# RWKV attention and a channel mixer in one kernel: three kinds of early VectorE work on GpSimd and ScalarE, and a weight request behind two products

## The chip, the cores and the metric

The kernel runs on one core of a Trainium2 chip. The metric is the device time of one execution in microseconds, lower is better. The engines are TensorE (PE; its weight loads are PEld), VectorE (DVE), ScalarE (ACT), GpSimd (POOL) and SyncE (SP), each with its own queue of instructions that it works through in order; they wait for each other by semaphores. Transfers are asked for by SyncE and GpSimd and run on 16 DMA engines.

## What is computed

A linear attention with a decaying state, and then an MLP mixer on its output, for 4 batches, 8 heads, 768 tokens and 48 elements per head (384 per token):

```python
for t in range(S):                                    # S = 768
    kt, vt, rt = (k[:, :, t], v[:, :, t], r[:, :, t])
    cur = np.einsum('bhd,bhe->bhde', u[None] * kt, vt)
    y[:, :, t] = np.einsum('bhd,bhde->bhe', rt, state + cur)
    state = w[None, :, :, None] * state + np.einsum('bhd,bhe->bhde', kt, vt)
...
xt = x.transpose(0, 2, 1)                             # x: y as (4, 768, 384)
h = np.maximum(xt @ w_tok1, 0.0) @ w_tok2             # 768 -> 256 -> 768 over the tokens
u = x + h.transpose(0, 2, 1)
h2 = np.maximum(u @ w_ch1, 0.0) @ w_ch2               # 384 -> 1536 -> 384 over the channels
return u + h2
```

## The kernel before

The tokens of each batch are cut into 6 units of 128, so there are 24 units; units 0 to 5 are the first batch. Attention within a unit is a product of scaled k and scaled r (the decay w is put into both by tables of its powers), masked to earlier tokens, times v; what came before the unit enters through a state matrix.

One unit u goes through these steps, each a short function that issues one or a few instructions:

- `kp`, `rp`: k and r, as loaded (`ld_k`, `ld_r`, f32 in SBUF), times their tables `wn` and `wp`, into the bf16 tile `kpr` (on GpSimd or VectorE). There are five such tiles, used in turn. `vb`: v as bf16 (ScalarE).
- `trk`, `trr`: four transposes each of the k half and the r half of `kpr`, into one PSUM tile `tr_ps` (TensorE).
- `rk`: `tr_ps` copied to SBUF (ScalarE). For units 0 to 4 and 6 it is two steps, `rkk` (k half, after `trk`) and `rkr` (r half, after `trr`); for others one step that issues both copies after `trr`.
- `at`: eight score matmuls into two PSUM tiles of four heads, `at_ps` 0 and 1 (TensorE). `AT0`, `AT1`: each of the two times the f32 mask, as bf16 into SBUF (VectorE). For units 0, 1, 5, 8 and 11 the second half goes another way: `raw` copies it from PSUM to bf16 (ScalarE), and `ATr` multiplies that by a bf16 mask (VectorE, both operands in SBUF).
- `pr`, `pg`, `yd`: the diagonal term (VectorE, four tiny matmuls into `g_ps`, VectorE or GpSimd). `pr` reads both halves of `rk`.
- `yS`, `y`: the state's part and the part within the unit, into `y_ps` (TensorE). `kv`, `S`: the state's update; in the third unit of a batch (unit 2 in the first) `S` uses the table `wGm`, which is built once from the constants `bm` and `wG`.
- `x`: `y_ps` plus `yd` into `x_b` (VectorE), the mixer's input.

When all six units of a batch are there, the mixer follows: `hid` and `hr` (token product and ReLU, `h_ps`, `h1r`), `ux`/`ub` or `bk`/`us` (second token product, added to x), then two halves of twelve `z` products with ReLU copies `zr` on ScalarE, and `h` products with `wch2`, `os` and the store. The `z` and `h` products of earlier batches are what TensorE does most of the time.

The order on each engine is not written by hand. `graph` makes all steps with their dependencies, ranks and estimated durations; `Plan.run` plays them through, gives each step an engine and a start, and sorts them; the kernel then issues them in that order. Two things are set behind it. `Plan.fill` puts idle matmuls (`fill_ps`) into TensorE's planned gaps. `products_in_turn` looks at the products of SBUF operands on VectorE and GpSimd, and where a GpSimd product stands at most 2.0 us behind one of VectorE's, it adds a wait of GpSimd's for VectorE. Every instruction passes through one helper, so the profile's line is the same for all, L515, and the tiles tell them apart; units are told by order.

The five weights come by seven GpSimd requests, which also turn f32 to bf16: `w0` and `w1` (the two token weights, tiles `wtok`), `w2`, `w6`, `w4` (first quarter, second quarter and second half of the columns of the first channel weight, `wch`), `w3` and `w5` (the second channel weight by halves of its rows). Their place on GpSimd is set by `wafter`. The loads of k, r and v stand on SyncE's queue; the first six units' are issued ahead of all else, and unit 6's k load waits for unit 5's y matmuls (`hold`).

Of the kernel before, what the change touches and what calls it, by code (L numbers as in the profile page):

```python
# [45 lines left out]
class Plan:  # L46
# [83 lines left out]
    def fill(self, since, until, least, margin, each, emit):  # L130

        mine = sorted((s for s in self.steps if s.engine == "PE"), key=lambda s: s.start)
        for a, b in zip(mine, mine[1:]):
            if b.start > until:
                break
            if a.end < since:
                continue
            taken = sum(1 for x in self.used if x[0] < b.start and x[1] > a.end)
            n = int((b.start - a.end - margin) / each)
            if b.start - a.end >= least and taken < self.banks and n > 0:  # L140
                s = self.add(f"fill{a.name}", [("PE", n * each, n * each)], emit=emit(n))
                s.engine, s.start, s.end, s.seen = "PE", a.end, a.end + n * each, a.end + n * each
        return sorted(self.steps, key=lambda s: s.start)


def products_in_turn(steps, apart):


    both = [s for s in steps if s.engine in ("DVE", "POOL") and s.name.rstrip("0123456789") in ("kp", "rp", "ku", "rku", "yd", "wGm")]
    dve = [s for s in steps if s.engine == "DVE"]  # L150
    behind, d = {}, None
    for s in both:
        if s.engine == "DVE":
            d = s if len(s.after) and s.name[:2] != "yd" or s.ways[0][0] == "POOL" else d
        elif d is not None and s.start - d.end < apart:
            n = dve.index(d)
            behind[s] = dve[n - 1] if n and d.start - dve[n - 1].end < 0.05 else d
            d = None
    return behind
# [9 lines left out]
def graph(do, cfg):  # L169
# [246 lines left out]
CFG = dict(apart=2.0,   # L416
    transfers=[("u", u) for u in range(0, 6)]
    + [('k', 6)]
    + [('r', 6)]
    + [('k', 7)]  # L420
    + [('r', 7)]
    + [('v', 6)]
    + [('v', 7)]
    + [('u', 8)]
# [20 lines left out]
    xload={6: 0.33},  # L445
    wtime=(3.0, 2.6, 1.55, 5.2, 3.1, 3.9, 1.55),
    raw=(0, 1, 5, 8, 11),
    rk_two=(0, 1, 2, 3, 4, 6),
    mix=(0.0, 0.0, -1.0, -2.6),
    off3=[{}, {}, {'AT0': -0.12, 'rp': 0.83, 'rku': 1.35}],  # L450
# [17 lines left out]
def kernel(  # L468
# [121 lines left out]
    for i in range(NB):  # L590
        t = const.tile([128, 2, H, P], bf16, name=f"kpr{i}")
# [24 lines left out]
    wGm = const.tile([128, HP, 2, D], f32, name="wGm")  # L616
# [387 lines left out]
    def do(kind, *args):  # L1004
        return lambda eng: STEPS[kind](eng, *args)

    def fill(eng, n):
        t = psM.tile([128, 512], f32, name="fill_ps", tag="m")
        for lo in range(0, n, 2):
            cols = slice(0, 256 * min(2, n - lo))  # L1010
            pe.matmul(t[:, cols], idle[:, 0:128], idle[:, cols], start=True, stop=True)

    plan = graph(do, CFG)
    steps = plan.run()
    if CFG.get("fill"):
        first = next(s for s in steps if s.name == "z0_0_0").start
        steps = plan.fill(CFG.get("fill_from", 0.0), first, *CFG["fill"], lambda n: lambda eng: fill(eng, n))
    behind = products_in_turn(steps, CFG["apart"])
    last = {}
    for s in steps:  # L1020
# [38 lines left out]
```

## Time and profile before

| | |
|---|---|
| Median of 3 runs | 165.36 us (164.93 to 165.66) |
| Profiled execution | 165.7 us, its span 164.0 us |
| Mean granted TensorE clock | 1.000 |
| Busy: TensorE / VectorE / ScalarE / GpSimd | 156.6 / 109.2 / 88.5 / 67.1 us |
| Moved by DMA | 26.26 MB, mean 160 GB/s |
| DMA packets under 512 B | 76665 of 87307 |

A row of the timeline reads: start and duration in us from the span's start, engine, line, operation, output<-inputs, shapes, how many in a row, and in brackets the idle time of the engine ahead of it and what ended it. The chain of waits has start, duration and what was waited for or done. In the page's slices one digit is a fortieth of the span, 4.1 us, and tells the busy tenths. A row of transfers tells the size of one and the time from its issue to its landing. A row of the windows tells the stretch, its length, the busy time of TensorE, its weight loads, VectorE, ScalarE and GpSimd (with the number of instructions), the granted clock, the DMA engines' busy share and GB/s.

### The profile page before, as it was taken

The numbers are of one execution on the slowest core, as the hardware profiler recorded it, in microseconds if no ns is written. First come the engines' busy times: TensorE is split into PE (matmuls) and PEld (weight loads), VectorE is DVE, ScalarE is ACT, GpSimd is POOL, SyncE is SP. The second block draws the span as 40 slices with busy tenths as digits, with TensorE's granted clock in tenths as the row PEclk, the third lists the DMA queues.
The fourth block names the chain that finished last, engine by engine and source line by source line (L and its number), as shares of the span: only waits on it lengthen the run. The fifth ranks groups of instructions, "written<-read, shape, count | busy, mean of one in ns | idle before, by whom it ended". The sixth has DMA issues, their size and how long they took to land.

```text
span 164.0 us, 3852 instructions
## 1 busy us (share of the span) xinstructions
PE 156.6 (95%) x1466; PEld 100.9 (62%) x1466; DVE 109.2 (67%) x225; ACT 88.5 (54%) x194; POOL 67.1 (41%) x83
## 2 busy tenths in 40 slices
PE   6798999999999999899999999999999999999992
PEld 3277865566677666566566565666656655666562
DVE  6679897602289889899899899977876582012021
ACT  3898662595488466789706450077253502914900
POOL 8748893000037848566875856204750000000000
DMA  4999999999798997999999972999990028012012
GB/s 92 221 223 207 173 154 173 192 194 232 153 231 233 190 213 220 196 238 180 217 231 133 263 135 67 203 231 194 194 240 4 0 53 216 19 52 96 0 48 96
DMA packets 87307, 26.26 MB, mean 160 GB/s; under 512 B 76665, under 2 KB 87290, under 8 KB 87290
## 3 DMA queue, kind: packets, MB, share of 16 engines
q1 hardware_dynamic: 83392, 22.88, 65.1%
q0 software_dynamic: 3888, 3.15, 13.1%
q8 instruction: 11, 0.18, 0.4%
q14 instruction: 6, 0.05, 0.2%
q10 hardware_dynamic: 10, 0.00, 0.0%
HBM read 20.65 MB, written 4.72 MB: 155 GB/s over the span
## 4 chain that ended last, share of the span: by engine, by line
PE 85%; DVE 5%; ACT 5%; issue 2%; POOL 1%; DVEq 0%; ACTq 0%
PE h_ps L515 33%; PE z_ps L515 29%; PE y_ps L515 5%; PE at_ps L515 5%; PE tr_ps L515 4%; PE hT_ps L515 3%; PE kv_ps L515 3%; ACT rk L515 2%; DVE AT L515 2%; DVE x_b L515 1%; PE w_ps L515 1%; DVE yd L515 1%; POOL kpr L515 1%; ACT wp L515 1%; ACT raw L515 1%
## 5 line engine op out<-in xcount | busy, mean ns | idle before, releaser
L515 ACT ACTIVATE zr<-z_ps 128x384 bf16<-128x384 f32 x94 | 45.4, 492 | 44.2 <-PE z_ps L515 44.1
L515 PE MATMUL z_ps<-uT,wch 128*128 128x384 bf16 x288 | 52.5, 326 | 0.2
L515 PE MATMUL h_ps<-wch,zr 128*128 128x384 bf16 (+1 forms) x300 | 52.5, 320 | 0.0
L515 PEld LDWEIGHTS <-zr 128*128 128x128 bf16 x300 | 27.9, 98 | 15.5 <-issue 0.2
L515 PEld LDWEIGHTS <-wch 128*128 128x128 bf16 x288 | 26.7, 98 | 16.1 <-issue 0.4
L515 POOL TENSOR_TENSOR yd<-vb,adg 128x384 f32<-128x384 bf16 x18 | 15.5, 859 | 42.2 <-ACT adg L515 25.1
L515 DVE TENSOR_TENSOR AT<-at_ps,mask 128x512 bf16<-128x512 f32 x43 | 27.9, 683 | 0.6 <-PE at_ps L515 0.5
L515 DVE TENSOR_TENSOR osb<-u_sb,h_ps 128x384 f32<-128x384 bf16 (+1 forms) x22 | 11.7, 532 | 23.5 <-PE h_ps L515 23.4
L515 POOL TENSOR_TENSOR kpr<-ld_r,wp 128x384 bf16<-128x384 f32 x16 | 17.0, 1064 | 5.3 <-DVE yd L515 2.2
L515 ACT COPY rk<-tr_ps 128x512 bf16<-128x512 bf16 x28 | 15.5, 589 | 5.5 <-PE tr_ps L515 5.1
L515 PEld LDWEIGHTS <-kpr 128*128 128x128 bf16 x192 | 13.6, 108 | 6.1 <-POOL kpr L515 2.6
L515 DVE TENSOR_TENSOR x_b<-y_ps,yd 128x384 bf16<-128x384 f32 x24 | 13.3, 552 | 5.8 <-PE y_ps L515 5.5
L515 POOL TENSOR_TENSOR kpr<-ld_k,wn 128x384 bf16<-128x384 f32 x15 | 15.5, 1031 | 2.1 <-PE z_ps L515 1.1
L515 PEld LDWEIGHTS <-rk 48*128 48x128 bf16 (+1 forms) x272 | 11.1, 100 | 6.4 <-issue 2.8
L515 PE MATMUL tr_ps<-ident,kpr 128*128 128x128 bf16 x112 | 12.3, 247 | 2.0 <-ACT rk L515 1.0
L515 ACT CAST vb<-ld_v 128x384 bf16<-128x384 f32 x24 | 12.3, 511 | 3.5 <-DMA ld_v<-in_v_dram 3.5
L515 DVE TENSOR_TENSOR u_sb<-x_b,hT_ps 128x384 bf16<-128x384 bf16 x21 | 10.4, 546 | 1.1 <-PE hT_ps L515 1.1
L515 PEld LDWEIGHTS <-wtok 128*128 128x128 bf16 x90 | 8.0, 98 | 4.8 <-issue 0.6
L515 PEld LDWEIGHTS <-AT 128*128 128x128 bf16 x192 | 8.6, 99 | 3.6 <-DVE AT L515 0.7
L515 PE MATMUL at_ps<-rk 48*128 48x128 bf16 x192 | 10.4, 233 | 0.4 <-ACT rk L515 0.4
L515 DVE TENSOR_TENSOR kpr<-ld_k,wn 128x384 bf16<-128x384 f32 x9 | 5.9, 658 | 7.0 <-DMA ld_k<-in_k_dram 7.0
L515 PE MATMUL h_ps<-x_b,wtok 128*128 128x384 bf16 x48 | 10.2, 326 | 0.1
(91 smaller groups left out, 154.2 us busy)
## 6 DMA issues: line engine op xcount, KB each, us to landing
ld_k<-in_k_dram SPq DMA_DIRECT2D x24, 192.0 KB, 3.6
ld_v<-in_v_dram SPq DMA_DIRECT2D x24, 192.0 KB, 3.7
out_dram<-osb SPq DMA_DIRECT2D x23, 192.0 KB, 2.5
ld_r<-in_r_dram SPq DMA_DIRECT2D x28, 96.0 KB, 3.2
ld_r<-in_r_dram SPq DMA_DIRECT2D x10, 192.0 KB, 3.8
wch<-in_moe_w_ch_dram POOLq DMA_DIRECT2D x3, 576.0 KB, 12.6
wtok<-in_moe_w_tok_dram POOLq DMA_DIRECT2D x2, 384.0 KB, 5.1
wch<-in_moe_w_ch_dram POOLq DMA_DIRECT2D x2, 288.0 KB, 5.6
```

Of the source, the lines that this page charges most:

```text
L515: ins = tc.keep_in_program_order(f(*args, **kw))
```

## The change

A new function `placed` edits the finished plan before it is issued; the planner's own numbers stay as they are, and so does the order of the steps that are not named.

```diff
+def placed(steps, do, moved, raw, apart):
+    named = {s.name: s for s in steps}
+    for u in raw:
+        s = Step(f"raw{u}", [], (), None, (), 0.0, do("raw", u))
+        s.engine, s.start = "ACT", named[f"at{u}"].end + 0.001
+        s.end = s.seen = s.start + 0.6
+        named[f"AT1_{u}"].emit = do("ATr", u)
+        steps.append(s)
+    for u in apart:
+        s = Step(f"rkk{u}", [], (), None, (), 0.0, do("rkk", u))
+        s.engine, s.start = "ACT", named[f"trk{u}"].end + 0.001
+        s.end = s.seen = s.start + 0.5
+        named[f"rk{u}"].emit = do("rkr", u)
+        steps.append(s)
+    for name, engine, other in moved:
+        s, t = named[name], named[other]
+        s.engine = engine
+        if s is not t:
+            s.start = s.end = s.seen = t.start - 1e-6
+    return sorted(steps, key=lambda s: s.start)
...
     raw=(0, 1, 5, 8, 11),
+    raw_too=(2, 3, 4),
+    rk_apart=(5,),
+    moved=(('kp2', 'POOL', 'kp2'), ('wGm', 'POOL', 'rp2'), ('i:w1', 'POOL', 'i:w2')),
...
+    steps = placed(steps, do, CFG["moved"], CFG["raw_too"], CFG["rk_apart"])
     behind = products_in_turn(steps, CFG["apart"])
```

So units 2, 3 and 4 take the way by `raw` and `ATr` for the second half of their scores; unit 5's two copies of `tr_ps` become two steps, the first right behind `trk5`; `kp2` and `wGm` leave VectorE for GpSimd; and the request `w1` stands right ahead of `w2`, behind unit 5's products. `products_in_turn` is called afterwards, so it sees `kp2` and `wGm` on GpSimd and not on VectorE. SyncE's queue stays as it was, and TensorE's instructions keep their order; only some of their waits change.

On GpSimd, in the first batch, there stood (`kpr_134` is unit 2's tile, `kpr_136` unit 3's, `kpr_138` unit 4's, `kpr_130` unit 5's; `wtok_160` is the second token weight):

```order
L515 TENSOR_TENSOR kpr_132<-ld_r,wp 128x2x4x48 [waits DMAHW7_49,DMAHW1_49,Activation_49]
L515 TENSOR_TENSOR kpr_134<-ld_r,wp 128x2x4x48 [waits DMAHW3_49,DMAHW5_49,DVE_49,Activation_49]
L515 TENSOR_TENSOR kpr_136<-ld_k,wn 128x8x48 [waits DMAHW6_49]
L515 TENSOR_TENSOR kpr_136<-ld_r,wp 128x2x4x48 [waits DMAHW7_49,DMAHW1_49,DVE_49]
L515 TENSOR_TENSOR kpr_138<-ld_k,wn 128x8x48 [waits DMAHW2_49]
L515 DMA wtok_159<-in_moe_w_tok_dram 128x6x256
L515 TENSOR_TENSOR kpr_138<-ld_r,wp 128x2x4x48 [waits DMAHW5_49,DMAHW3_49]
L515 DMA wtok_160<-in_moe_w_tok_dram 128x2x768
L515 TENSOR_TENSOR kpr_130<-ld_k,wn 128x8x48 [waits DMAHW7_49,PE_49,Pool_49]
L515 TENSOR_TENSOR kpr_130<-ld_r,wp 128x2x4x48 [waits DMAHW0_49,DMAHW6_49,PE_49,Pool_49]
L515 DMA wch_161<-in_moe_w_ch_dram 128x3x384 x2
```

and now stands:

```order
L540 TENSOR_TENSOR kpr_132<-ld_r,wp 128x2x4x48 [waits DMAHW7_49,DMAHW1_49,Activation_49]
L540 TENSOR_TENSOR kpr_134<-ld_k,wn 128x8x48 [waits DMAHW2_49,Activation_49]
L540 TENSOR_TENSOR wGm<-bm,wG 128x384 [waits Activation_49]
L540 TENSOR_TENSOR kpr_134<-ld_r,wp 128x2x4x48 [waits DMAHW3_49,DMAHW5_49,DVE_49,Activation_49]
L540 TENSOR_TENSOR kpr_136<-ld_k,wn 128x8x48 [waits DMAHW6_49]
L540 TENSOR_TENSOR kpr_136<-ld_r,wp 128x2x4x48 [waits DMAHW7_49,DMAHW1_49]
L540 TENSOR_TENSOR kpr_138<-ld_k,wn 128x8x48 [waits DMAHW2_49]
L540 DMA wtok_159<-in_moe_w_tok_dram 128x6x256
L540 TENSOR_TENSOR kpr_138<-ld_r,wp 128x2x4x48 [waits DMAHW5_49,DMAHW3_49]
L540 TENSOR_TENSOR kpr_130<-ld_k,wn 128x8x48 [waits DMAHW7_49,PE_49,Pool_49]
L540 TENSOR_TENSOR kpr_130<-ld_r,wp 128x2x4x48 [waits DMAHW0_49,DMAHW6_49,PE_49,Pool_49]
L540 DMA wtok_160<-in_moe_w_tok_dram 128x2x768
```

Unit 2's k product and `wGm` came in ahead of unit 2's r product, unit 3's r product lost its wait for VectorE, and `wtok_160` went behind unit 5's two products.

On ScalarE, from the r half of unit 4's copy on, there stood (`at_ps_553` is unit 5's second score tile):

```order
L515 COPY rk<-tr_ps 128x512 [waits PE_49]
L515 CAST S_1_150<-kv_ps 48x4x48 [waits PE_49,Activation_49]
L515 CAST S_1_150<-kv_ps 48x4x48 [waits Activation_49]
L515 COPY rk<-tr_ps 128x512 [waits DVE_49,PE_49]
L515 COPY rk<-tr_ps 128x512
L515 CAST vb<-ld_v 128x384 [waits DMAHW1_49,DVE_49]
L515 CAST raw<-at_ps_553 128x512 [waits DVE_49,PE_49]
```

and now, from the new copy ahead of it (`at_ps_446` is unit 3's tile, `at_ps_504` unit 4's, `at_ps_559` unit 5's):

```order
L540 CAST raw<-at_ps_446 128x512 [waits DVE_49,PE_49]
L540 COPY rk<-tr_ps 128x512 [waits PE_49]
L540 CAST S_1_150<-kv_ps 48x4x48 [waits PE_49]
L540 CAST S_1_150<-kv_ps 48x4x48
L540 CAST raw<-at_ps_504 128x512 [waits DVE_49,PE_49]
L540 COPY rk<-tr_ps 128x512 [waits PE_49] x2
L540 CAST vb<-ld_v 128x384 [waits DMAHW1_49]
L540 CAST raw<-at_ps_559 128x512 [waits DVE_49,PE_49]
```

Units 3 and 4 each put a `raw` copy in; unit 5's two copies now wait for TensorE each by itself. With that, the first matmul of `trr5` waits for ScalarE, which it did not before: the transposes of the r half write the same PSUM tile that `rkk5` reads.

On VectorE, for unit 3, there stood:

```order
L515 TENSOR_TENSOR AT_466<-at_ps_443,mask 128x512 [waits PE_49]
L515 TENSOR_TENSOR AT_482<-at_ps_444,mask 128x512 [waits PE_49]
L515 TENSOR_TENSOR yd<-vb,g_ps 128x384 [waits PE_49]
L515 TENSOR_TENSOR pr<-tr_ps,rk 128x512 [waits Activation_49]
L515 TENSOR_TENSOR x_b_163<-y_ps,yd 128x384 [waits DVE_49,PE_49]
```

and now:

```order
L540 TENSOR_TENSOR AT_469<-at_ps_445,mask 128x512 [waits PE_49]
L540 TENSOR_TENSOR AT_485<-raw,mask_b 128x512 [waits Activation_49]
L540 TENSOR_TENSOR yd<-vb,g_ps 128x384 [waits PE_49]
L540 TENSOR_TENSOR pr<-tr_ps,rk 128x512 [waits Activation_49]
L540 TENSOR_TENSOR x_b_163<-y_ps,yd 128x384 [waits DVE_49,PE_49]
```

The second of them now reads `raw` and the bf16 mask, both in SBUF, and waits for ScalarE.

## The prediction

> **What bounds the kernel now.** I read the page first (busy time, slices, chain), then the chain of waits in order of time around the first batch, then the timelines of the engines there, then the transfers.
>
> ```profile
> PE 156.6 (95%) x1466; PEld 100.9 (62%) x1466; DVE 109.2 (67%) x225; ACT 88.5 (54%) x194; POOL 67.1 (41%) x83
> PE   6798999999999999899999999999999999999992
> DMA  4999999999798997999999972999990028012012
> ```
>
> TensorE is busy 95% of the span, and nearly every slice after the seventh (28.7 us) reads 9: behind the first batch the kernel is TensorE's own stream. So an early change is worth what it moves the point at which TensorE gets into the first long run of z products. The DMA row is full from the second slice to the tenth, so what is asked for there comes later for something else. The chain of waits says who sets that point:
>
> ```profile
> 11.80 0.42 ACT wp L515
> ...
> 13.91 0.59 PE tr_ps L515 x4
> ...
> 18.89 0.33 PE y_ps L515 x8
> ...
> 19.24 0.56 DVE x_b L515
> 19.80 1.27 DVE AT L515 x2
> ...
> 23.99 0.34 DVE pr L515
> ...
> 24.49 0.56 DVE x_b L515
> ...
> 26.55 0.57 DVE x_b L515
> ```
>
> Up to 19.2 us the chain runs over ScalarE and TensorE; only from 19.24 to 27.1 is it VectorE's. VectorE work taken away before 19.24 has a limit beside it that stays.
>
> **VectorE's part.** Two products go to GpSimd, and three of the f32 masked copies (AT out of at_ps) become ScalarE's copy plus a bf16 product.
>
> ```profile
> 10.64 0.55 DVE L515 TENSOR_TENSOR kpr<-ld_k,wn 128x384 bf16<-128x384 f32 x1
> 14.69 0.55 DVE L515 TENSOR_TENSOR wGm<-bm,wG 128x384 f32<-128x384 f32 x1
> L515 DVE TENSOR_TENSOR AT<-at_ps,mask x43: 675/681/693, 11.1 to 127.4; 128x512 bf16<-128x512 f32 x43
> L515 DVE TENSOR_TENSOR AT<-raw,mask_b x5: 415/415/417, 12.2 to 63.4; 128x512 bf16<-128x512 bf16 x5
> ```
>
> VectorE sheds 0.55 + 0.55 + 3 × (0.68 - 0.42) = 1.9 us. Of this kp2, wGm and unit 2's copy, 1.36 us, lie before 19.24 and are booked at nothing: the cover is ScalarE's and TensorE's chain of the fence above. Units 3 and 4, 0.26 us each, lie on the chain, so the gross gain is 0.52 us at x3 and x4.
>
> **What it costs on ScalarE.** Raw4 stands ahead of unit 5's two copies, and these are now divided.
>
> ```profile
> 22.58 1.07 ACT L515 COPY rk<-tr_ps 128x512 bf16<-128x512 bf16 x2 [1.23 <-PE tr_ps L515]
> 24.33 0.59 ACT L515 CAST raw<-at_ps 128x512 bf16<-128x512 f32 x1 [0.26 <-PE at_ps L515]
> 21.41 0.40 PE L515 MATMUL at_ps<-rk 48*128 48x128 bf16 x8
> 22.14 0.40 PE L515 MATMUL tr_ps<-ident,kpr 128*128 128x128 bf16 x4
> ```
>
> With VectorE 0.25 us earlier, at4 starts at 21.2 and ends at 21.6. Raw4 runs 21.6 to 22.2; the first copy, as long as raw's, 22.1 to 22.7; trr5 now waits for it (the new wait in the order), so it runs 22.7 to 23.1 with unit 4's y products and at5 queued behind it on TensorE; the second copy runs 23.15 to 23.75, against 23.65 before. pr5, which needs it, starts at 23.78 instead of 23.90. Of the 0.52 us some 0.1 is left at x5, because unit 5's copies are late next. ScalarE's three new copies, 0.47 us of queue each, lie otherwise in its idle time (1.23 us in the row above). So alone this part is worth -0.1 us.
>
> **What it costs on GpSimd.**
>
> ```profile
> 9.08 0.99 POOL L515 TENSOR_TENSOR kpr<-ld_r,wp 128x384 bf16<-128x384 f32 x1
> 12.31 1.13 POOL L515 TENSOR_TENSOR kpr<-ld_r,wp 128x384 bf16<-128x384 f32 x1 [2.24 <-DVE yd L515]
> 14.85 1.25 POOL L515 TENSOR_TENSOR kpr<-ld_r,wp 128x384 bf16<-128x384 f32 x1 [0.46 <-DVE AT L515]
> 18.37 0.99 POOL L515 TENSOR_TENSOR kpr<-ld_r,wp 128x384 bf16<-128x384 f32 x1 [0.48 <-DMA ld_r<-in_r_dram]
> 19.32 0.78 POOL L515 DMA_DIRECT2D wtok<-in_moe_w_tok_dram  x1
> 20.12 1.02 POOL L515 TENSOR_TENSOR kpr<-ld_k,wn 128x384 bf16<-128x384 f32 x1
> 21.08 1.01 POOL L515 TENSOR_TENSOR kpr<-ld_r,wp 128x384 bf16<-128x384 f32 x1
> ```
>
> kp2 and wGm (no row of wGm on GpSimd; between 0.99 and the 1.25 of the slowest product here, taken at 1.0) fill the 2.24 us before rp2, 10.07 to 12.1: nothing, and +0.2 us at worst if both take 1.25. rp3 loses its wait on VectorE, so it and the first token weight's request come 0.5 us earlier; rp4 still waits for its load. Then kp5 runs 19.33 to 20.3 and rp5 20.29 to 21.3, 0.8 us earlier, which in itself is worth nothing (trk5 is held by TensorE's queue, not by kp5).
>
> But rp5 now stands beside a new VectorE product. Unit 3's bf16 product is ready when AT0 of unit 3 is done, 19.78 + 0.61 = 20.39, and reads two operands from SBUF. What happens then is seen further on in the kernel:
>
> ```profile
> 63.55 0.99 POOL L515 TENSOR_TENSOR yd<-vb,adg 128x384 f32<-128x384 bf16 x1
> 63.77 1.18 DVE L515 TENSOR_TENSOR kpr<-ld_k,wn 128x384 bf16<-128x384 f32 x1
> 19.78 1.29 DVE L515 TENSOR_TENSOR AT<-at_ps,mask 128x512 bf16<-128x512 f32 x2
> ```
>
> A VectorE product of two SBUF operands that came 0.22 us behind a GpSimd product took 1.18 us instead of 0.55: it ended 0.41 us after GpSimd did. No row has the bf16 product (0.42 us alone) behind one of GpSimd's, so its price lies between nothing and the whole rest of rp5; I take the whole, since the f32 row is the nearest. The Trainium skill ("SBUF — State Buffer", section "SBUF: two separate sides") has a rule for it: VectorE's operation with two SBUF inputs and a GpSimd operation that reads SBUF need one port pair as an exclusive lock, and whichever starts first holds it for the whole instruction. By that rule the bf16 form waits as well (+0.58), by the bf16 rows alone it would wait for nothing (-0.1 in all); the trace agrees for the f32 form (1.18 against 0.55), and no run here shows the bf16 one.
>
> By the f32 row: the product ends at about 21.29 + 0.36 = 21.65 (0.36 for 0.41, since the bf16 form is the shorter), against 19.78 + 1.29 = 21.07 before: +0.58. yd3, pr4 and x3 queue behind it, y3 and at4 wait for it, so at4, raw4, the divided copies and pr5 all start some 0.6 to 0.7 us later than before (unit 4's 0.26 is eaten by the divided copies). At x5 I take +0.6.
>
> **The weights.** The second token weight is asked for at 21.25 instead of 19.32; the channel weights' requests stay at 22.03 onward, one behind the other.
>
> ```profile
> wtok<-in_moe_w_tok_dram POOLq DMA_DIRECT2D x1, 384.0 KB, 5.3
> wtok<-in_moe_w_tok_dram POOLq DMA_DIRECT2D x1, 384.0 KB, 4.8
> wch<-in_moe_w_ch_dram POOLq DMA_DIRECT2D x1, 288.0 KB, 5.3
> wch<-in_moe_w_ch_dram POOLq DMA_DIRECT2D x1, 576.0 KB, 9.3
> 24.00:25.00 1.00, 1.00 (x17) 0.64 (x14) 0.83 (x3) 0.65 (x2) 1.00 (x2) 1.00 0.73 45
> 27.00:28.00 1.00, 0.89 (x6) 0.38 (x4) 0.41 (x3) 0.32 (x2) 0.00 (x0) 1.00 1.24 196
> 27.87 0.94 PE L515 MATMUL at_ps<-wtok,h1r 128*128 128x384 bf16 x4
> 31.82 6.99 PE L515 MATMUL z_ps<-uT,wch 128*128 128x384 bf16 x42
> ld_k<-in_k_dram SPq DMA_DIRECT2D x1, 192.0 KB, 4.3
> ```
>
> From issue to landing they took 5.3 and 4.8 us (token weights, issued 17.00 and 19.32), 5.3 (first channel part, 22.03) and 9.3 (the third part, issued 23.60, so landed at 32.9). The second token weight itself moved in about 19.32 + 4.8 - (17.00 + 5.3) = 1.8 us. It now stands in front of the channel weights in a stream that was nearly full. If it fills the hole of 24 to 25 us (45 GB/s where 196 is usual) the delay is about 0; if the hole only moves behind it, 1.8 us. Landing at 21.25 + 4.8 to 5.3 = 26.0 to 26.6 and the first part 1.5 us (288 KB at 196 GB/s) behind it gives 27.5 to 28.1 against 27.3: I take 0.5. The token weight has time (its first reader is at 27.9). The third part is the tight one: the seventh z group reads it 12 matmuls into the run, 31.82 + 12 × 6.99/42 = 33.8, so 0.8 us of cover counting the weight load. 0.5 is hidden.
>
> **Sum**, against the profiled execution's 165.7 us (span 164.0): -0.1 for VectorE and ScalarE, +0.7 for the wait behind rp5, 0 for the weights: 166.3. The three runs' median, 165.36, lies 0.34 below that execution, so I forecast 166.0 for the runs: +0.6, or 0.4%, inside the 0.5% (0.83 us) that a measurement of this kernel can tell.
>
> **Rivals.**
> *VectorE gets in ahead of rp5.* The margin is 0.1 us (20.39 against 20.29). The first token weight, asked for 0.5 us earlier, shares the DMA engines with unit 5's k load (last row of the fence above: issued 14.80, landed 4.3 us later at 19.1), only 0.2 us before kp5 can start; 0.2 to 0.4 us more and kp5 is still running at 20.39, VectorE goes between it and rp5, and ends within 0.1 us of before. Then -0.1 to +0.2: 165.4. Chance 0.32; the case above 0.36.
> *The weights are late, slower than before.* Every 0.1 us that the third part comes later than its 0.8 us of cover is 0.1 us of TensorE standing still in the z run. rp5 held behind VectorE would put all requests another 0.4 to 0.6 us back. A hole that stays (1.8 us) gives 1.8 - 0.8 = +1.0, with the later requests +1.5: 166.4 to 166.9. For it: the DMA row; against it: the hole is there to be filled. It decides from 1.6 us of delay on. Chance 0.24.
> *The 1.9 us of VectorE come through.* If unit 5's copies and TensorE's order gave way, the batch could end 1 to 1.5 us earlier; but then TensorE reaches the third channel part 0.8 us before it landed, and nothing makes that part earlier than now. So -0.8 at most, 164.5, unless the hole vanishes as well. Chance 0.08.
>
> Of the first case a fifth or so, where other delays add to it, passes +0.83; with the weights' case 0.30 for slower. Faster by over 0.5%: 0.07, nearly all of the last. The rest, 0.63, is within. The likeliest case's own range is 165.8 to 166.3; 165.0 to 166.8 leaves out the last rival and the far end of the third.
>
> **What would show it.** Right: the bf16 product of unit 3 lasting about 1.2 us at 20.4 beside rp5; ScalarE's row of two copies near 22.6 torn in two with a wait on tr_ps between; x5 at about 27.2; the token weight landing near 26 and no wait on wch in the z run. Wrong: that product at 0.42 us and x5 at 26.5 (second case), a gap of TensorE at the seventh z group that ends with a DMA (third), x5 before 26.0 (fourth). GpSimd's kp2 or wGm running past 12.3 would spoil the early part.

## The result, and the profile after

The changed kernel takes 166.63 us (median of 7 runs, 165.91 to 166.97) against 165.60 us before (7 runs, 164.93 to 165.67): a ratio of 1.0064, with a 95% interval of 1.0043 to 1.0085. It is 1.03 us slower, just beyond the 0.83 us that count as a difference here. The ratios in this document are worked out over the runs, without those that lie over 1.5% above the fastest of their kernel, so they are not the ratios of the medians. The profiled execution took 166.62 us, its span 164.9 us (164.0 before).

```profile
PE 156.7 (95%) x1466; PEld 100.8 (61%) x1466; DVE 109.8 (67%) x223; ACT 90.2 (55%) x197; POOL 68.7 (42%) x85
```

VectorE has two instructions fewer and yet 0.6 us more busy time (109.2 before): some of its instructions got longer. The chain of waits of the changed kernel (start, duration, what) says which. From 9.39 to 15.00 us it now runs over VectorE, where that of the kernel before runs over ScalarE and TensorE:

```profile
9.59 0.51 DVE UW L540
10.10 0.01 issue
10.11 0.95 DVE UW L540
...
12.58 0.64 DVE AT L540
...
22.54 0.58 ACT raw L540
23.12 0.50 ACT rk L540
23.62 0.04 issue
23.66 0.38 PE tr_ps L540 x4
```

`UW` is a pair of tiny products of two SBUF operands, 64 partitions by 4 elements (the weights of the diagonal term). The timelines of VectorE and GpSimd in the changed kernel show what stood beside them:

```profile
9.59 1.47 DVE L540 TENSOR_TENSOR UW<-wu_sb 64x4 bf16<-64x4 f32 x2
12.49 1.10 DVE L540 TENSOR_TENSOR AT<-raw,mask_b 128x512 bf16<-128x512 bf16 x1
17.82 0.99 DVE L540 TENSOR_TENSOR AT<-raw,mask_b 128x512 bf16<-128x512 bf16 x1
21.14 0.43 DVE L540 TENSOR_TENSOR AT<-raw,mask_b 128x512 bf16<-128x512 bf16 x1
```

```profile
10.05 0.99 POOL L540 TENSOR_TENSOR kpr<-ld_k,wn 128x384 bf16<-128x384 f32 x1
11.00 0.82 POOL L540 TENSOR_TENSOR wGm<-bm,wG 128x384 f32<-128x384 f32 x1
12.32 1.00 POOL L540 TENSOR_TENSOR kpr<-ld_r,wp 128x384 bf16<-128x384 f32 x1 [0.50 <-ACT wp L540]
...
17.50 1.01 POOL L540 TENSOR_TENSOR kpr<-ld_r,wp 128x384 bf16<-128x384 f32 x1
...
20.01 1.00 POOL L540 TENSOR_TENSOR kpr<-ld_r,wp 128x384 bf16<-128x384 f32 x1
20.95 0.77 POOL L540 DMA_DIRECT2D wtok<-in_moe_w_tok_dram  x1
```

The second `UW` product came to its turn at 10.11, 0.06 us after unit 2's k product had started on GpSimd (10.05), and lasted until that product had ended (11.04): 0.95 us. In the kernel before, where no GpSimd product ran then, it took 0.16 of the pair's 0.69:

```profile
9.58 0.69 DVE L515 TENSOR_TENSOR UW<-wu_sb 64x4 bf16<-64x4 f32 x2
```

```profile
10.10 0.16 DVE L515 TENSOR_TENSOR UW<-wu_sb 64x4 bf16<-64x4 f32 x1
```

The first product of the pair was held in both kernels (0.51 us in the chain above), behind unit 1's r product, which ended at 10.07 and 10.08. So VectorE was 0.80 us late at unit 0's `pr`. That put unit 0's bf16 product (12.49) behind unit 2's r product (12.32), where it had been ahead of it before (12.16 against 12.31): 1.10 us instead of 0.42. Later unit 2's new bf16 product stood behind unit 4's r product, 0.99. Unit 3's, which the prediction had named, came at 21.14, after that r product of unit 5 had ended (21.01), and took 0.43. The score products on TensorE give the ledger of what is late:

```profile
15.81 0.61 PE L515 MATMUL at_ps<-rk 48*128 48x128 bf16 x8
...
19.14 0.61 PE L515 MATMUL at_ps<-rk 48*128 48x128 bf16 x8
```

```profile
16.52 0.61 PE L540 MATMUL at_ps<-rk 48*128 48x128 bf16 x8
...
19.84 0.61 PE L540 MATMUL at_ps<-rk 48*128 48x128 bf16 x8
...
22.07 0.40 PE L540 MATMUL at_ps<-rk 48*128 48x128 bf16 x8
...
23.66 0.38 PE L540 MATMUL tr_ps<-ident,kpr 128*128 128x128 bf16 x4 [0.79 <-ACT rk L540]
...
32.75 6.99 PE L540 MATMUL z_ps<-uT,wch 128*128 128x384 bf16 x42
```

The first fence is before, the second after: unit 2 is 0.71 us late, unit 3 0.70, unit 4 0.66 (21.41 before). From 15.04 to 22.51 the chain of waits stands on TensorE alone. Then unit 5 loses more, at the divided copies:

```profile
24.70 0.42 DVE L540 TENSOR_TENSOR pr<-tr_ps,rk 128x512 bf16<-128x512 bf16 x1 [0.48 <-ACT rk L540]
27.47 0.56 DVE L540 TENSOR_TENSOR x_b<-y_ps,yd 128x384 bf16<-128x384 f32 x1 [0.42 <-PE y_ps L540]
```

`pr` of unit 5 is 0.80 late (23.90), `x` of unit 5 0.92 (26.55), the long run of z products 0.93 (31.82), and the span ends 0.9 later. That run stands in one piece of 42: no weight was waited for.

### The profile page after: what moved, and what is told of

It reads as the page before. It is cut to its first block, busy times and chain, and to the rows that moved or that the text cites. A ratio compares the mean times of both kernels' runs of the same rounds, so it can differ in the third digit from the quotient of the medians.

```text
span 164.9 us, 3850 instructions
## 1 busy us (share of the span) xinstructions
PE 156.7 (95%) x1466; PEld 100.8 (61%) x1466; DVE 109.8 (67%) x223; ACT 90.2 (55%) x197; POOL 68.7 (42%) x85
## 4 chain that ended last, share of the span: by engine, by line
PE 88%; DVE 5%; ACT 3%; issue 2%; POOL 1%; DVEq 0%; ACTq 0%
PE h_ps L540 34%; PE z_ps L540 29%; PE y_ps L540 6%; PE at_ps L540 5%; PE tr_ps L540 4%; PE hT_ps L540 3%; PE kv_ps L540 3%; ACT rk L540 1%; PE w_ps L540 1%; PE fill_ps L540 1%; DVE AT L540 1%; DVE UW L540 1%; POOL kpr L540 1%; ACT vb L540 1%; PE t_ps L540 1%
## 5 line engine op out<-in xcount | busy, mean ns | idle before, releaser
L540 DVE TENSOR_TENSOR AT<-at_ps,mask 128x512 bf16<-128x512 f32 x40 | 26.2, 683 | 0.6 <-PE at_ps L540 0.5
L540 POOL TENSOR_TENSOR kpr<-ld_k,wn 128x384 bf16<-128x384 f32 x16 | 16.9, 1054 | 2.7 <-PE z_ps L540 1.1
L540 PE MATMUL y_ps<-vb,AT 128*128 128x48 bf16 x192 | 9.3, 188 | 0.3 <-DVE AT L540 0.3
```

The costliest lines, as they stand in the source:

```text
L540: ins = tc.keep_in_program_order(f(*args, **kw))
```

## The experiments

Twelve kernels, each against the kernel before on the same chip. `at2` is the start of unit 2's score products in the profiled execution (15.81 before, 16.52 in the changed kernel), the last point that all profiles reach at the same matmul rate. `x` of unit 5 lies behind it and carries up to 0.8 us that differ from one execution to the next (see the last section).

| | median us | ratio to before (95%) | at2 | x of unit 5 |
|---|---|---|---|---|
| changed kernel | 166.63 | 1.0064 (1.0043 to 1.0085) | 16.52 | 27.47 |
| 1 no products moved to GpSimd | 165.82 | 1.0026 (1.0007 to 1.0046) | 15.91 | 27.47 |
| 2 UW from PSUM | 166.17 | 1.0038 (1.0023 to 1.0053) | 15.75 | 26.68 |
| 3 before + kp2 on GpSimd | 166.08 | 1.0037 (1.0021 to 1.0053) | 16.46 | 26.68 |
| 4 copies of unit 5 not divided | 166.18 | 1.0041 (1.0023 to 1.0060) | 16.52 | 26.98 |
| 5 all blamed waits out | 165.58 | 1.0002 (0.9979 to 1.0024) | 15.78 | 26.49 |
| 6 before + UW from PSUM | 165.71 | 0.9999 (0.9983 to 1.0015) | 15.80 | 26.55 |
| 7 as 1, without unit 3's raw | 165.89 | 1.0009 (0.9987 to 1.0031) | 15.76 | 25.82 |
| 8 before + later token weight | 165.69 | 1.0004 (0.9984 to 1.0024) | 15.79 | 26.00 |
| 9 as 2 and 4 together | 166.32 | 1.0053 (1.0027 to 1.0079) | 15.76 | 27.10 |
| 10 before + divided copies | 165.40 | 0.9999 (0.9976 to 1.0021) | 15.77 | 26.01 |
| 11 before + earlier token weight | 165.81 | 1.0013 (0.9989 to 1.0038) | 15.87 | 26.61 |
| 12 as 5, earlier token weight | 166.47 | 1.0024 (0.9996 to 1.0052) | 15.76 | 27.01 |

**1. The two products back on VectorE.**

```diff
-    moved=(('kp2', 'POOL', 'kp2'), ('wGm', 'POOL', 'rp2'), ('i:w1', 'POOL', 'i:w2')),
+    moved=(('i:w1', 'POOL', 'i:w2'),),
```

> The changed kernel with unit 2's k product and wGm back on VectorE; the three bf16 score products, unit 5's divided copies and the later token weight stay. Theory (the 0.9 us come from VectorE's products of two SBUF operands standing behind GpSimd's, first of all the two tiny UW products behind unit 2's k product): the UW pair is back at 0.69 us (1.47 now), unit 0's bf16 product at 0.42 (1.10), x of unit 2 starts at 19.0 to 19.3 (19.95), and the time falls by 0.5 to 0.9 us to 165.7 to 166.1; if rp5 then stands at 20.3 just ahead of unit 3's bf16 product (20.39), that one takes about 1.2 us and the time stays at 166.1 to 166.3. Rival (ScalarE's three more copies and their place in its queue cost the time): x of unit 2 still at 19.9 and 166.5 to 166.7.

165.82 us. The timelines of VectorE, of GpSimd and of TensorE (this execution's first steps all lie 0.1 us later than before's):

```profile
9.70 0.68 DVE L540 TENSOR_TENSOR UW<-wu_sb 64x4 bf16<-64x4 f32 x2
12.28 0.42 DVE L540 TENSOR_TENSOR AT<-raw,mask_b 128x512 bf16<-128x512 bf16 x1
...
20.53 1.20 DVE L540 TENSOR_TENSOR AT<-raw,mask_b 128x512 bf16<-128x512 bf16 x1
```

```profile
20.44 1.00 POOL L540 TENSOR_TENSOR kpr<-ld_r,wp 128x384 bf16<-128x384 f32 x1
```

```profile
15.91 0.61 PE L540 MATMUL at_ps<-rk 48*128 48x128 bf16 x8
...
22.07 0.40 PE L540 MATMUL at_ps<-rk 48*128 48x128 bf16 x8
```

`UW` and unit 0's bf16 product are short again and `at2` is back. And with VectorE on time, unit 3's bf16 product does stand 0.09 us behind unit 5's r product and takes 1.20 us: at4 starts at 22.07, 0.56 later than before after taking off the 0.1. The rival (ScalarE's copies) would have left `at2` late; it falls. The 12 runs lie between 165.51 and 166.8, the profiled one, 166.61, near the top: the other runs may not all pay this wait.

**2. `UW` with one operand from PSUM.** The k product stays on GpSimd at 9.99.

```diff
-            dve.tensor_mul(UW[half, :, q], wu_sb[half, 0, :], wu_sb[half, 1, :])
+            dve.tensor_mul(UW[half, :, q], wu_sb[half, 0, :], M0["wu"][half, 1, :])
```

> The changed kernel with one edit: the two UW products read one of their two operands from the PSUM tile it was copied from, so they no longer read two SBUF operands; unit 2's k product stays on GpSimd at 10.05. Theory (lock): the UW pair ends by 10.0 although the GpSimd product runs from 10.05, pr of unit 0 starts at or before 10.29 (11.09), unit 0's bf16 product at 12.2 or earlier with 0.42 (1.10), x of unit 2 at 19.0 to 19.4. What follows: either unit 3's bf16 product then meets rp5 (20.0 to 21.0) and the time stays at 166.2 to 166.6, or it does not and only unit 5's divided copies are left, 165.7 to 166.0. Rival (GpSimd's k product itself, or its later wGm and rp2, hold the chain): UW short, but x of unit 2 still at 19.9, time 166.5 to 166.7.

166.17 us. The timelines of VectorE and GpSimd:

```profile
9.53 0.33 DVE L540 TENSOR_TENSOR UW<-wu_sb,wu_ps 64x4 bf16<-64x4 f32 x2
...
11.69 0.42 DVE L540 TENSOR_TENSOR AT<-raw,mask_b 128x512 bf16<-128x512 bf16 x1
...
20.13 0.81 DVE L540 TENSOR_TENSOR AT<-raw,mask_b 128x512 bf16<-128x512 bf16 x1
```

```profile
9.03 0.99 POOL L540 TENSOR_TENSOR kpr<-ld_r,wp 128x384 bf16<-128x384 f32 x1
9.99 0.99 POOL L540 TENSOR_TENSOR kpr<-ld_k,wn 128x384 bf16<-128x384 f32 x1
```

Unit 1's r product (9.03 to 10.02) runs beside the whole pair, as it ran beside the first `UW` product of the changed kernel, and holds it no more: the pair takes 0.33 us and is done at 9.86, before unit 2's k product starts. What held it was its second SBUF operand. `at2` is 15.75 with unit 2's two products and `wGm` still on GpSimd, so the rival falls. The median fell by 0.46 and not by 0.7: unit 3's bf16 product now stood behind unit 5's k product (0.81), and the divided copies are still in.

**3. Before, with unit 2's k product alone on GpSimd.**

```diff
-    raw_too=(2, 3, 4),
-    rk_apart=(5,),
-    moved=(('kp2', 'POOL', 'kp2'), ('wGm', 'POOL', 'rp2'), ('i:w1', 'POOL', 'i:w2')),
+    raw_too=(),
+    rk_apart=(),
+    moved=(('kp2', 'POOL', 'kp2'), ),
```

> The kernel before with only unit 2's k product moved to GpSimd (VectorE 0.55 us lighter). Theory (lock): the UW pair takes about 1.47 us, pr of unit 0 starts at 11.1 (10.29); VectorE, 0.8 later and 0.46 relieved, reaches unit 1's pr some 0.3 us late (12.8), rp2 waits for the later yd (12.6 instead of 12.31), x of unit 2 at 19.4 to 19.6: 0.1 to 0.4 us slower than before, 165.7 to 166.0. Rival (the lock at UW costs nothing since ScalarE and TensorE bind): x of unit 2 at 19.2 and 165.5 to 165.7; or the 0.55 us of VectorE come through and it is 0.3 faster.

166.08 us: this one move, which takes 0.55 us off VectorE, makes the kernel 0.37% slower. `UW` took 1.46, unit 0's bf16 product 1.10, `at2` started at 16.46. One expectation was wrong: the r product of unit 2 didn't wait for the later `yd` (it started at 12.26, released by ScalarE's `wp`), so the second collision came too, and the time lies 0.1 above the expected range. That `x` of unit 5 is only 0.13 us late in this profile goes with TensorE's faster rate, which came at 18.0 us here and at 19.8 before. The run also shows what lies behind: a gap in the z run that a weight ends.

```profile
34.28 0.99 PE L540 MATMUL z_ps<-uT,wch 128*128 128x384 bf16 x5 [0.21 <-DMA wch<-in_moe_w_ch_dram]
```

**4. Unit 5's copies not divided.**

```diff
-    rk_apart=(5,),
+    rk_apart=(),
```

> The changed kernel with unit 5's two copies of tr_ps again as one step. Theory (the divided copies cost a second piece: trr5 waits for rkk5, which stands behind unit 4's raw copy): trr5 starts at about 22.8 (23.66), the two copies run as a pair from 23.1 to 24.2, pr of unit 5 starts at 24.2 (24.70), x of unit 5 at 26.9 to 27.1 (27.47), and the time falls by 0.3 to 0.5 us to 166.1 to 166.3. Rival (dividing them is worth what it was made for, or nothing): 166.6 or more, x of unit 5 at 27.4 or later.

166.18 us, as expected. `trr5` starts at 22.96 without a wait (23.66), `pr` of unit 5 at 24.54, `x` at 26.98. From at4 (22.29) to `pr` it takes 2.25 us, in the changed kernel 24.70 - 22.07 = 2.63. at4 itself is 0.22 us later than there, since here unit 3's bf16 product did meet unit 5's r product, on VectorE and GpSimd:

```profile
20.88 1.08 DVE L540 TENSOR_TENSOR AT<-raw,mask_b 128x512 bf16<-128x512 bf16 x1
```

```profile
20.68 0.99 POOL L540 TENSOR_TENSOR kpr<-ld_r,wp 128x384 bf16<-128x384 f32 x1 [0.16 <-PE kv_ps L540]
```

**5. All blamed waits out.** Edits 2 and 4 together; in addition only unit 4 by `raw`, and the token weight where it was. Two products more on GpSimd than before remain.

```diff
-    raw_too=(2, 3, 4),
-    rk_apart=(5,),
-    moved=(('kp2', 'POOL', 'kp2'), ('wGm', 'POOL', 'rp2'), ('i:w1', 'POOL', 'i:w2')),
+    raw_too=(4,),
+    rk_apart=(),
+    moved=(('kp2', 'POOL', 'kp2'), ('wGm', 'POOL', 'rp2'), ),
...
-            dve.tensor_mul(UW[half, :, q], wu_sb[half, 0, :], wu_sb[half, 1, :])
+            dve.tensor_mul(UW[half, :, q], wu_sb[half, 0, :], M0["wu"][half, 1, :])
```

> The changed kernel with everything taken out that the theory blames: the UW products read one operand from PSUM, only unit 4 (not 2 and 3) takes the way by raw and the bf16 product, unit 5's copies of tr_ps are one step, and the second token weight is asked for where it was before. Unit 2's k product and wGm stay on GpSimd. Theory: no VectorE product of the first batch is longer than 0.7 us, x of unit 2 starts at 18.9 to 19.2 (19.24 before the change, 19.95 after), unit 4's half of 0.26 us comes through, x of unit 5 at 26.0 to 26.4 (26.55 and 27.47), and the time is 165.0 to 165.5 unless the third part of the first channel weight (32.9) now ends last. Rival (GpSimd's added products or the three more ScalarE copies cost by themselves, lock or not): 165.9 or more.

165.58 us: the loss is gone, but no gain takes its place (165.0 to 165.5 was expected, and the rival's 165.9 falls). VectorE's busy time is 1.3 us less than before (107.9 against 109.2), and `x` of unit 5 starts at 26.49, since `trr5` waits for GpSimd, whose r product of unit 5 ran at 21.40:

```profile
22.45 0.40 PE L540 MATMUL tr_ps<-ident,kpr 128*128 128x128 bf16 x4 [0.45 <-POOL kpr L540]
```

**6. Before, with `UW` from PSUM.** Edit 2 on the kernel before.

> The kernel before with one edit: the two UW products read one operand from PSUM. Theory: they already stood behind rp1 in the kernel before (0.69 us for the pair, 0.33 without), so the pair takes 0.33 and pr of unit 0 starts at 9.9 (10.29); but up to x of unit 2 ScalarE and TensorE bind, so x of unit 2 moves by 0.2 at most (19.0 to 19.24) and the time by 0 to -0.2: 165.4 to 165.6. Rival (VectorE binds from the start): 0.36 faster, 165.2.

165.71 us, no change, though `UW` took 0.33 instead of 0.69 and `pr` of unit 0 began 0.36 us earlier. The kernel before paid 0.36 us there too, behind unit 1's r product, and at a place where ScalarE and TensorE cover it: `at2` stayed at 15.80.

**7. As 1, without unit 3's `raw`** (`raw_too=(2, 4)`).

> The kernel of the first experiment (unit 2's k product and wGm on VectorE, later token weight, divided copies) without unit 3's bf16 product: units 2 and 4 alone take that way. Theory (there rp5 at 20.44 held that product to 1.20 us instead of 0.42, and not in every execution): both halves of unit 3 run as a pair of 1.29 us at 19.9 with rp5 beside them, x of unit 3 at 21.9 (22.45), x of unit 5 at 26.8 to 26.9 (27.47) with the divided copies still in, every execution like the faster ones of that experiment (165.5 to 166.0), median 165.5 to 165.7. Rival (the copies or the weights, not rp5, made its slow executions): median 165.8 and single executions up to 166.8 as there.

165.89 us. `x` of unit 5 came as early as 25.82, most of it by TensorE's faster rate, which came at 16.8 us here (`x` of unit 2 at 18.26, 19.24 before). The end is not earlier (the z run ends at 38.82, 38.81 before), because the third part of the channel weight ends a wait in that run:

```profile
33.77 1.47 PE L540 MATMUL z_ps<-uT,wch 128*128 128x384 bf16 x8 [0.28 <-DMA wch<-in_moe_w_ch_dram]
```

The theory fails for the time: with unit 3's wait out, the median is no lower than in experiment 1, near the rival's 165.8, though no single run is as slow (166.55 at most). So these runs do not show what unit 3's wait cost in the median of experiment 1; in how many executions it stands was not seen.

**8. Before, with the later token weight alone.**

```diff
-    raw_too=(2, 3, 4),
-    rk_apart=(5,),
-    moved=(('kp2', 'POOL', 'kp2'), ('wGm', 'POOL', 'rp2'), ('i:w1', 'POOL', 'i:w2')),
+    raw_too=(),
+    rk_apart=(),
+    moved=(('i:w1', 'POOL', 'i:w2'),),
```

> The kernel before with only the second token weight's request moved behind unit 5's two products on GpSimd. Theory (weights cost nothing): kp5 and rp5 0.8 us earlier, no wait on wch at the seventh z group, x of unit 5 within 0.1 of 26.55, 165.4 to 165.7. Rival (the channel weight's third part comes too late): a gap of TensorE at about 34 us that a DMA ends, 166.0 to 166.9. Other rival (an earlier rp5 is worth something): 165.2 or less.

165.69 us: nothing, as expected. In the profile `x` of unit 5 began at 26.00 (expected 26.55). Unit 5's products came 1.07 us earlier on GpSimd (20.01), but TensorE's faster rate also came earlier, at about 18.0 us, and `x` of unit 2, which does not need those products, was 0.46 early already (18.78). A weight load in the z run waited 0.34 us for the third part, which made the run 0.13 us longer (7.12 us, 6.99 before); this one execution was still 0.4 us shorter (span 163.6).

**9. Edits 2 and 4 together.**

> The changed kernel with two edits together: the UW products read one operand from PSUM, and unit 5's copies of tr_ps are one step. Unit 2's k product and wGm on GpSimd, the bf16 products of units 2 to 4 and the later token weight stay. Theory (the first edit alone took off 0.46 us of the median, the second alone 0.45, and they lie at different places of the chain): together 0.7 to 0.9 us off, 165.7 to 165.9; unit 2's score products start at 15.8 (16.52 in the changed kernel, 15.81 before). Rival (a third cost is left: rp5 in front of unit 3's bf16 product, as seen at 20.53 in the first experiment): 166.0 to 166.2. Other rival (both edits remove the same wait): 166.1 to 166.2, with unit 5's x no earlier than with the first edit alone.

166.32 us, not 165.8. `at2` is 15.76 as expected, but in this profile, one of the slowest executions (167.29 us; the runs go from 165.47 to 167.75), the second half of unit 5's r load was late. SyncE's queue, GpSimd and TensorE:

```profile
15.76 1.56 SPq L540 DMA_DIRECT2D ld_r<-in_r_dram  x1
```

```profile
22.01 1.00 POOL L540 TENSOR_TENSOR kpr<-ld_r,wp 128x384 bf16<-128x384 f32 x1 [1.88 <-PE g_ps L540]
```

```profile
23.07 0.40 PE L540 MATMUL tr_ps<-ident,kpr 128*128 128x128 bf16 x4 [1.12 <-POOL kpr L540]
```

That load's issue took 1.56 us instead of 0.6 and it landed at 21.8 (19.4 before), though the row puts the wait down to TensorE. In experiment 12 it happened as well (issue 1.37, product at 21.91). Issues of that length are not new: before and in the changed kernel the v load asked for next took 1.39 and 1.51 us, and in experiment 10 it was again this r load (1.37), which landed at 20.4 and held nothing up. The first token weight had been asked for at 16.34 and 16.44 in experiments 9 and 12, and at 17.00 before; but also at 16.27 in experiment 5, where the load was in time. How often the load is late, and why, stays open, and so does whether the two edits would add with the load in time.

**10. Before, with the divided copies alone** (`raw_too=()`, `moved=()`).

> The kernel before with only unit 5's two copies of tr_ps divided. No raw copy of unit 4 stands ahead of them here. Theory (it was raw of unit 4 that made the first copy late): the first copy starts when trk5 is done, at 22.0 to 22.1, trr5 waits for it until 22.7, the second copy ends at 23.7 as the pair did (23.65): x of unit 5 at 26.5 to 26.7 and 165.4 to 165.8. Rival (dividing costs by itself, since TensorE's queue stands behind trr5 while the first copy runs): 0.4 us slower, 166.0. Other rival (it is a gain): 165.2 or less.

165.40 us, no change: both rivals fall. From at4 (20.77) to `pr` of unit 5 (23.24) it takes 2.47 us, 2.49 before: dividing costs nothing where no `raw` of unit 4 stands ahead of the first copy. `x` of unit 5 came at 26.01 and not at 26.5 to 26.7, as TensorE's faster rate came at 16.8 us here.

**11. Before, with the second token weight right behind the first** (`moved=(('i:w1', 'POOL', 'rp4'),)`, the rest off).

> The kernel before with only the second token weight's request moved the other way: right behind the first one, ahead of unit 4's r product, where GpSimd waits for that r load. Theory (in the runs with the later request x of unit 5 came 0.55 to 0.73 us earlier, and the third part of the first channel weight, landing at 33.2 to 33.9, then took it back): rp5 ends at 21.1 to 21.7 (22.09), all requests of the channel weights start as much earlier, the third part lands by 32.5 without a wait at the seventh z group, x of unit 5 at 26.0 to 26.4, 0.1 to 0.5 us faster, 165.1 to 165.5. Rival (the token weight's packets delay the r and k loads of units 4 and 5): rp4 at 18.7 or later and no change or slower, 165.6 to 166.0.

165.81 us, no gain, as its rival has it: unit 5's r product started at 20.61 (21.08), and `x` of unit 5 at 26.61.

**12. The same on experiment 5.**

> The kernel without the blamed waits (UW products with one operand from PSUM, only unit 4 by raw, unit 5's copies as one step, unit 2's k product and wGm on GpSimd) and with the second token weight asked for right behind the first one. Theory: GpSimd, free 0.7 us earlier in this form, has rp5 done at 20.9 to 21.6, x of unit 5 at 25.7 to 26.2 (26.55 before), the third channel part lands by 32.4, and the time is 164.8 to 165.3, faster than both. Rival (loads late through the token weight's packets, or TensorE's rate up to 20 us binds anyway): 165.4 to 165.8, the same as before.

166.47 us, above both expectations, with runs from 164.44 to 169.74. One run is the fastest of all, most are slower than before. In the profiled one unit 5's r load was late (experiment 9). No version beat the kernel before.

## Why the prediction was right or wrong

The forecast was 166.0 us, no measurable change but slower; it came out 166.63, inside the range, beyond the likeliest case's 165.8 to 166.3 and the 0.83 us. The mechanism of the main term was right, its place was wrong: the wait booked behind rp5 at +0.7 did not come, and a wait of the same kind at `UW`, which the prediction did not have, cost 0.71 us at `at2`. That the two are of one size, and the time near the forecast, is luck.

- **"Fill the 2.24 us before rp2: nothing, and +0.2 us at worst"** is the step that failed. The two products did end in that gap (11.82), faster than taken (0.82 for `wGm`). But the step asked only who waits for them, not which VectorE product of two SBUF operands comes due beside them, though the `UW` pair of before, 0.69 us for two products of which the second took 0.16, showed that such a tiny product is held. One of 0.16 us did come due, and pushed unit 0's bf16 product into the next collision: the whole +0.71 at `at2` is there, and experiments 2 and 3 show it from both sides.
- **The price, "+0.58", behind rp5**: right where it happened, in experiment 1 (1.20 us long, at4 0.56 late); it happened in experiment 4 too (1.08). In the changed kernel it did not happen: VectorE was already 0.7 us late, and rp5 ended 0.13 us before unit 3's product was due. rp5 was also 0.28 us earlier than the 20.29 worked out, since "rp4 still waits for its load" was wrong (17.50, without a wait); at the time worked out it would have ended at 21.29, and the product at 21.14 would have met it. That the bf16 form is held like the f32 one, which no row of before showed, is shown by 1.10, 0.99 and 1.20 us against 0.42. This is the rule of the Trainium skill ("SBUF — State Buffer", section "SBUF: two separate sides"), an exclusive lock for the whole instruction; experiment 2 agrees also on its condition, two SBUF inputs.
- **"Booked at nothing"** for kp2, `wGm` and unit 2's copy: right. Experiment 5 keeps the two moves without the waits, and `at2` doesn't move (15.78 against 15.81). Experiment 1 keeps unit 2's copy, and unit 3's score products start at 19.24, which after taking off the 0.1 is the 19.14 of before.
- **The divided copies**: worked out as 2.58 us from at4 to `pr` of unit 5 (21.2 to 23.78), measured 2.63 against 2.49 before. But the net -0.1 was wrong. The 0.52 us of units 3 and 4 did not come through: VectorE was 0.21 us less late at `x` of unit 3 (0.50, 22.28 against 21.78), but the chain of waits stood on TensorE there, and unit 4's score products were only 0.05 less late (0.66 against 0.71). From there to `x` of unit 5 0.26 us were lost (0.92 late). So in these two profiles this part cost 0.21 us.
- **The other rivals**: VectorE did not get in ahead of rp5, it came behind it; and nothing of the 1.9 us came through.
- **The weights, 0**: right. The third part landed at about 33.2 (32.9), and the run waited for nothing, although the requests did not "stay at 22.03" (21.72). The rival of a late weight falls for this kernel; in experiments 3 and 7 such a wait does appear (0.21 and 0.28 us).
- **"Nothing makes that part earlier than now"**, written against the fourth rival: borne out. In experiments 7 and 8 `x` of unit 5 came 0.73 and 0.55 us earlier, and weight loads waited for that part until 33.77 and 33.33. It took back all of it in experiment 7 and 0.13 us in experiment 8; neither median moved.
- **The median**: 0.34 us was taken off because three runs had the median 165.36. Over 7 runs it was 165.60 and over 35 it was 165.59 to 165.72, so about 0.3 of the missing 0.6 us is this, and the other 0.3, by the profiles, the copies (+0.21 for -0.1).

The parts' medians do not add (experiments 2, 4, 9), and their intervals overlap; what is shown is the wait at `UW` and its 0.7 us at `at2`, that one move with this wait makes the kernel slower (experiment 3), and that the loss goes with all the waits (experiment 5), not a split of the 1.03 us to a tenth.

## What to carry to other kernels

Before a product goes to GpSimd, list every VectorE instruction with two SBUF operands that can come due while it runs, however small, and price each at the rest of the GpSimd product; in experiment 2, giving one operand from PSUM took the wait away. Making VectorE 1.3 us lighter was worth nothing here, as the next limits stood close behind: GpSimd's own chain (experiment 5), ScalarE's order (experiment 4) and the landing of a weight (experiment 7). When one wait is removed, look which near miss it turns into a collision.

## What the runs showed of the hardware

A VectorE product of 64x4 elements was held 0.95 us by a GpSimd product that had started 0.06 us earlier; nothing in the profile names this wait, the instruction just gets longer.

TensorE's matmuls change their rate in the first batch, at a moment that differs by execution. Before, and in experiment 7:

```profile
19.14 0.61 PE L515 MATMUL at_ps<-rk 48*128 48x128 bf16 x8
```

```profile
18.15 0.40 PE L540 MATMUL at_ps<-rk 48*128 48x128 bf16 x8
```

Eight score products take 0.61 us up to that moment and 0.40 behind it. The moment lay between 16.8 (experiments 7 and 10) and 20.9 us (the changed kernel), at 19.8 before. The windows of the changed kernel show a granted clock of 1.00 (the third number from the end) on both sides of it, with TensorE busy throughout (the third number):

```profile
19.00:20.00 1.00, 1.00 (x15) 0.66 (x15) 0.66 (x3) 0.89 (x3) 0.95 (x1) 1.00 1.02 134
20.00:21.00 1.00, 1.00 (x19) 0.80 (x16) 1.00 (x2) 0.68 (x2) 1.00 (x3) 1.00 1.34 174
```

So the profile's `x` of units 2 to 5 carry up to 0.8 us of luck (`x` of unit 2 came at 18.41 in experiment 10 and at 19.24 before, with `at2` at 15.77 and 15.81), and only the medians, or points ahead of the change as `at2`, compare kernels. Of the 0.9 us between the two profiles of the result little can be this: counted from `at2`, the moment came 4.0 us later before and 4.4 in the changed kernel, and 0.4 us at 0.61 for 0.40 cost 0.14 us (an estimate from these rows). The Trainium skill ("TensorE: Matmul & The Clock Gate", section "Part 1: The HAM clock gate (the "warmup" mystery)") has a clock gate that opens after a busy window of about 3.4 us, and the window runs freely, so the moment depends on where in it the work starts. By that figure it would open one to two windows after TensorE became busy, 3.4 to 6.8 us (an estimate from the page's figure). Here TensorE had been busy from about 14 us on, with pauses of at most 0.22 us, so the change came 2.8 to 6.9 us later, which roughly agrees. The run-to-run scatter of 0.5 us that the same section gives is far less than the 4.1 us here. That it is this gate, no run shows.
